# Turning the identity on TensorE ahead of the first keys, which come in two loads and are scored in two parts

## The chip, the core and the metric

The kernel runs on one core of a Trainium2 chip. The metric is the device time of one execution in microseconds (us); the lower the better.

## What is computed

Eight batches, eight heads of width 64, 576 tokens. A packed query p of 32 rows for each head first attends over the keys and values; then the 576 queries q attend over the 32 packed rows. The result, 4608 tokens by 512, goes through a feed-forward net with an ELU between its two matrices.

```python
def sm_attn(qq, kk, vv):
    s = scale * np.matmul(qq, kk.transpose(0, 1, 3, 2))
    s = s - np.max(s, axis=-1, keepdims=True)
    a = np.exp(s)
    a = a / (np.sum(a, axis=-1, keepdims=True) + 1e-09)
    return np.matmul(a, vv)
p_packed = sm_attn(p, k, v)            # (8, 8, 32, 64)
out = sm_attn(q, p_packed, p_packed)   # (8, 8, 576, 64)
x = out.transpose(0, 2, 1, 3).reshape(4608, 512)
h = x @ w_in                           # (4608, 2048)
g = np.where(h > 0.0, h, np.exp(np.minimum(h, 0.0)) - 1.0)
return (g @ w_out).astype(np.float32)
```

The weights arrive as float64, two 32-bit words each, and the kernel makes float32 of them.

## The kernel before

The work is written as some thousands of small steps. Each is an `op(prio, on, fn, deps, take, use, after)`: a priority, the engines that can do it with a cost for each, the function that issues its instructions, the steps it needs, the buffers that it takes and uses. `schedule()` is a planner: it plays the steps through in its own time with these costs, each time the first step in order of priority whose needs and buffers are there, and so fixes for every engine the order of its instructions. The instructions then stand on their engine's queue in that order, and each waits for what it needs. SP's queue issues nearly all loads.

The names that matter here, with the lines of the kernel before:

- `weights(f, first, prio)` turns one block of float64 weights into float32. Load `raw` (L305; three buffers, so the fourth load waits until the first block is used up), then on DVE `exponent` (L310), `mantissa` (L325), `whole` (L331), `signed` (L338) and `product` (L348), on ACT `sign` (L322) and `power` (L317). Blocks of the first matrix are called i0, i1, ..., of the second o0, o1, ... The blocks o0 to o3 are kept in `w_words` and later split into a high part (ACT, L282, CAST `wo_a`) and a low part (DVE, L361).
- `attention(b, ts)` is one batch. Loads of p and the keys (L459, L461 for batch 0, L463 for the others), the values (L470, L474) and the queries (L480, L482). Keys, values and queries of the batches after the first take turns in the same pairs of buffers (`kvq`), so that the queries of batch 1 are loaded when the values of batch 1 are used up.
- In it `s1` scores the packed queries (PE, L511). `smax1` (DVE, L521), `neg` (L529), `sexp1` (ACT, L535) and `srec1` (L543, L546) are its softmax, `tr1` turns it (PE, L622), ACT copies it (L282), `pv` multiplies by the values (PE, L648), `norm` scales (L660), and `tr2` (PE, L674) and a copy on ACT give `ppT`.
- `s2` scores one half of the queries against `ppT` (PE, L693). On DVE `fold` (L701), `smax` (L708), `ssub` (L711), on ACT `sexp` (L717), on DVE `ssum` (L721), `srec` (L724, L727), `smul` (L730) and `unfold` (L743) make the attention weights of that half.
- `mstep` multiplies `ppT` by the first matrix (PE, L794, copied by ACT as `m_hi`).
- The large matmuls of the net: L1263 and L1270 give a block of h (its first ones read what L743 wrote and `m_hi`), ACT and DVE make g of it (L1277, L1283, L1286), L1380 and L1394 to L1397 multiply it by the second matrix. In the later batches L1036 and L1175 do the same in another form.

The constants set priorities: `T_ATT1` the steps of batch 1 against the large matmuls, `LI`, `LO`, `LM` how long ahead weights and `mstep` come, `T_S2` the scores of batch 0's queries, `T_WS` the splitting of o0 to o3, `T_AS` the splitting of the first batches' attention weights. `FIRST` is the order of the first loads.

Of the kernel before, what the change touches and what calls it, by code (L numbers as in the profile page):

```python
# [20 lines left out]
def packed_attention_elu_ffn(  # L21
# [22 lines left out]
    nc = tc.nc  # L44
    B, P, NPAIR, S = qT.shape
# [32 lines left out]

    T_ATT, T_ATT1 = [12, 14.0, 14.5, 15.5, 16.5, 16.5], [-12, -11, -11, -10, -10, -9]
    LI, LO, LM, LOOK = 4.5, 3.0, 2.5, 3.5
    TM = [24.5, 22.0, 25.0, 25.5]

    FIRST = "i0 i1 i2 i3 k v o0 o1 q".split()
    T_S2, STAY, SWITCH = 0, 4, 0.12

    F_PLAIN, H_PLAIN = 4, [0, 1]  # L90
    T_WS, T_AS = 20, 6

# [64 lines left out]
    def op(prio, on, fn, deps=(), take=(), use=(), after=(), mode=None, lag=0):  # L159
        o = Op()  # L160
        o.lag = lag
        o.prio, o.on, o.fn, o.deps = prio, on, fn, [d for d in deps if d is not None]
        o.after = [d for d in after if d is not None]
        o.take, o.end, o.n, o.mode = list(take), None, len(ops), mode
        for b in list(take) + list(use):
            b.users.append(o)
        ops.append(o)
        return o
# [71 lines left out]
    ident = const.tile([P, P + 16], F32, name="ident")[:, 16:]  # L240
# [20 lines left out]
    def banks(n):  # L261
        b = Buf(R["psum"], lambda: psum[:, b.at, :] if n == 1 else psum[:, b.at:b.at + n, :], n)
        return b
# [137 lines left out]
    def attention(b, ts):  # L401
# [55 lines left out]
        def load_k(e, n):  # L457
            if n == 0:
                nc.sync.dma_start(out=p_b.t, in_=pT[b])  # L459
            if b == 0:  # L460
                nc.sync.dma_start(out=k_b[0].t, in_=kT[b])  # L461
            else:
                nc.sync.dma_start(  # L463
                    out=k_b[n].t[:, :2 * S].rearrange("p (c s) -> p c s", c=2),
                    in_=kT[b, :, 2 * n:2 * n + 2, :],
                )
# [21 lines left out]
        for name, fn, bufs, t in (  # L488
            ("k", load_k, k_b, ts[0] - 6), ("v", load_v, v_b, ts[0] - 5), ("q", load_q, q_b, ts[0] - 3),
        ):  # L490
            lds[name] = []
            if b == 0:
                t = FIRST.index(name) - 60
            for n, x in enumerate(bufs):
                prev_ld = op(
                    t, {"DMA": (3.3 if b < 3 else 3.8) / len(bufs)}, lambda e, fn=fn, n=n: fn(e, n),
                    take=[x] + ([p_b] if (name, n) == ("k", 0) else []), after=[prev_ld],
                    lag=1.5 * (b > 2),
                )
                lds[name].append(prev_ld)  # L500
        ld_k, ld_v, ld_q = lds["k"], lds["v"], prev_ld
# [2 lines left out]
        ps1, e1s = [banks(2) for _ in range(G)], [temp() for _ in range(G)]  # L504
        sv = {}

        def s1(e):
            for half in range(2):
                for pair in range(NPAIR):
                    for g in range(G):  # L510
                        nc.tensor.matmul(  # L511
                            ps1[g].t[cols_of(pair), half, :HS],
                            lhsT=p_b.t[rows_of(g), pair, :],
                            rhs=keys(pair)[rows_of(g), half * HS:(half + 1) * HS],
                            start=True, stop=True,
                        )
# [66 lines left out]

        o4s, o, t, free = [], None, ts[0], prev_b.tmp_last if b > 1 else None
        if b < S_FIRST[0] + 1:
            o1 = op(t, {"PE": 1.0}, s1, ld_k, take=ps1 + e1s, use=[p_b] + k_b, after=[free], mode=1)
            for g in range(G):
                o = op(t, {"DVE": 0.76}, lambda e, g=g: smax1(e, g), [o1], use=[ps1[g]], after=[o])
                o = op(t, {"DVE": 0.16}, lambda e, g=g: neg(e, g), [o])
                o4s.append(op(  # L590
                    t, {"ACT": 0.95}, lambda e, g=g: sexp1(e, g), [o], use=[ps1[g], e1s[g]],
                ))
        else:
            kept, o1 = [], None
            for half in range(2):
                ps = ps1[half]
                o1 = op(
                    t, {"PE": 0.52}, lambda e, half=half, ps=ps: s1_half(e, half, ps), ld_k,
                    take=[ps] + (e1s if half == 0 else []), use=[p_b] + k_b + e1s * half,
                    after=[free, o1], mode=1,  # L600
                )
                o = op(t, {"DVE": 0.76}, lambda e, half=half, ps=ps: smax1_half(e, half, ps), [o1],
                       use=[ps], after=[o])
                kept += [op(
                    t, {"ACT": 0.4}, lambda e, half=half, ps=ps, g=g: keep(e, half, ps, g), [o1],
                    use=[ps, e1s[g]],
                ) for g in range(G)]
            o = op(t, {"DVE": 0.26}, neg_both, [o])
            for g in range(G):
                o4s.append(op(  # L610
                    t, {"ACT": 0.9}, lambda e, g=g: sexp1_flat(e, g), [o] + kept[g::G], use=[e1s[g]],
                ))
# [398 lines left out]
    def strassen_pair(i, b, win, f):  # L1011
# [180 lines left out]
        if last:  # L1192
# [45 lines left out]

            op(q, {"DMA": 1.4}, store, [y], use=[part])

    acc = None
    for i, (b, win, f) in enumerate(order):
        st = sts[b]
# [252 lines left out]
```

## Time and profile before

| | |
|---|---|
| median of 3 runs | 713.93 us (713.62 to 714.21) |
| the profiled execution | 714.56 us, of which the span from the first to the last instruction is 712.4 us |
| busy share of the span | PE 97%, PEld 80%, DVE 81%, ACT 62%, POOL 3% |
| chain that ended last | PE 93%, DMA 3%, DVE 2%, ACT 1% |
| mean granted TensorE clock | 0.998 |

PE is TensorE's matmul and PEld its weight load, DVE VectorE, ACT ScalarE, POOL GpSimd and SP the queue that issues loads. The profile is one execution, so its rows add up to its own 714.56 us. A row of the timeline has start, length, engine, line, operation and tiles, and in brackets how long the engine was idle before it and what ended that. A row of the chain has start, length and what ran. Matmuls are pipelined, so the length of one (some 400 ns) is more than its share of a row of many.

### The profile page before, as it was taken

The page shows a single profiled execution, that of the slowest core. Times are in us where ns is not written, and L with a number is a line of the kernel's source. Part 1 is how long each engine was busy: PE and PEld are TensorE (multiplying, and loading weights), DVE is VectorE, ACT ScalarE, POOL GpSimd, SP SyncE. Part 2 cuts the span into 40 slices and gives each one's busy share as a digit, 9 for nine tenths or more (in the row PEclk, how much of TensorE's full clock was granted, in tenths as well). Part 3 has the DMA queues.
Part 4 walks back from the last instruction along what each step waited for, and adds up shares of the span by engine and source line. Part 5 has one row for each costly group of instructions (what it writes and reads, how often), then busy time and mean ns, then how long its engine had stood idle before and what let it go on. Part 6 is the DMA issues. An engine that isn't in the chain of part 4 may idle for free.

```text
span 712.4 us, 14951 instructions
## 1 busy us (share of the span) xinstructions
PE 689.7 (97%) x5616; PEld 572.2 (80%) x5616; DVE 576.4 (81%) x1405; ACT 442.2 (62%) x952; POOL 19.5 (3%) x27
## 2 busy tenths in 40 slices
PE   2799999999999999999999999999999999999997
PEld 1454588887778888988888988889888998899986
DVE  6999998888998899776996789776797789886553
ACT  5777788886666566665556455656556455655432
POOL 0000002111021000000000000000000000000000
PEclk9999999999999999999999999999999999999999
DMA  9846555545748836538577784627857874644400
GB/s 352 289 152 216 169 172 120 141 82 126 212 104 216 276 127 188 167 121 254 197 226 232 243 298 146 203 78 241 269 164 225 256 244 133 226 133 124 158 31 29
DMA packets 67368, 130.74 MB, mean 184 GB/s; under 512 B 6624, under 2 KB 16096, under 8 KB 67040
## 3 DMA queue, kind: packets, MB, share of 16 engines
q1 hardware_dynamic: 64272, 124.28, 53.6%
q0 software_dynamic: 3024, 5.51, 5.2%
q8 instruction: 44, 0.72, 0.4%
q14 instruction: 28, 0.23, 0.1%
HBM read 108.53 MB, written 21.23 MB: 182 GB/s over the span
## 4 chain that ended last, share of the span: by engine, by line
PE 93%; DMA 3%; DVE 2%; ACT 1%; issue 0%; SPq 0%; ACTq 0%
PE psum L1175 29%; PE psum L1036 18%; PE psum L1270 8%; PE psum L1394 5%; PE psum L1395 5%; PE psum L1397 5%; PE psum L995 5%; PE psum L794 4%; PE psum L1380 4%; PE psum L1263 2%; PE psum L648 1%; PE psum L622 1%; PE psum L693 1%; DMA out<-part 1%; DMA k<-in_kT 1%; PE psum L552 1%
## 5 line engine op out<-in xcount | busy, mean ns | idle before, releaser
L1175 PE MATMUL psum<-sw,g 128*128 128x256 f32 x720 | 112.3, 284 | 0.2
L1175 PEld LDWEIGHTS psum<-sw,g 128*128 128x128 f32 x720 | 96.7, 189 | 8.4 <-issue 6.4
L1036 PE MATMUL psum<-a_hi,m_hi 128*128 128x320 f32 (+1 forms) x320 | 96.9, 303 | 0.0
L1036 PE MATMUL psum<-a_lo,m_hi 128*128 128x320 f32 (+1 forms) x320 | 95.4, 298 | 0.0
L1036 PE MATMUL psum<-a_hi,m_lo 128*128 128x320 f32 (+1 forms) x320 | 95.3, 298 | 0.0
L282 ACT CAST g<-w 128x896 fp32r<-128x896 f32 (+1 forms) x80 | 68.6, 859 | 37.7 <-DVE w L1109 19.9
L1118 DVE TENSOR_TENSOR g<-w,g 128x896 fp32r<-128x896 f32 (+1 forms) x80 | 78.7, 985 | 16.1 <-ACT g L282 15.4
L1175 PE MATMUL psum<-wo_b,g 128*128 128x256 f32 (+1 forms) x390 | 72.7, 317 | 0.0
L1175 PE MATMUL psum<-wo_a,g 128*128 128x256 f32 (+1 forms) x390 | 72.2, 317 | 0.0
L1036 PEld LDWEIGHTS psum<-a_hi,m_hi 128*128 128x128 f32 x320 | 60.4, 189 | 11.3 <-issue 4.3
L1048 ACT ACTIVATE e<-psum 128x320 f32<-128x320 f32 x96 | 41.4, 436 | 43.4 <-PE psum L1036 33.9
L1277 ACT ACTIVATE e<-psum 128x256 f32<-128x256 f32 (+1 forms) x96 | 38.6, 403 | 46.9 <-PE psum L1270 32.9
L1175 PEld LDWEIGHTS psum<-wo_a,g 128*128 128x128 f32 x390 | 58.6, 188 | 7.7 <-issue 1.3
L1175 PEld LDWEIGHTS psum<-wo_b,g 128*128 128x128 f32 x390 | 58.5, 188 | 7.0 <-issue 2.6
L1109 DVE TENSOR_TENSOR w<-w 128x128 f32<-128x128 f32 x180 | 60.0, 334 | 4.4
L1036 PEld LDWEIGHTS psum<-a_lo,m_hi 128*128 128x128 f32 x320 | 60.4, 189 | 2.2
L1036 PEld LDWEIGHTS psum<-a_hi,m_lo 128*128 128x128 f32 x320 | 60.5, 189 | 0.0
L1043 DVE SCALAR_TENSOR_TENSOR w<-e,psum 128x256 f32<-128x256 f32 x96 | 39.7, 414 | 16.0 <-ACT e L1051 15.3
L1270 PE MATMUL psum<-a_hi,m_hi 128*128 128x256 f32 (+1 forms) x160 | 49.1, 307 | 0.0
L1286 DVE SCALAR_TENSOR_TENSOR e<-e,psum 128x256 f32<-128x256 f32 (+1 forms) x80 | 33.9, 425 | 16.1 <-ACT e L1283 15.9
L1270 PE MATMUL psum<-a_lo,m_hi 128*128 128x256 f32 (+1 forms) x160 | 46.4, 290 | 0.0
L1270 PE MATMUL psum<-a_hi,m_lo 128*128 128x256 f32 (+1 forms) x160 | 46.4, 290 | 0.0
(140 smaller groups left out, 1442.6 us busy)
## 6 DMA issues: line engine op xcount, KB each, us to landing
sw<-sw_dram SPq DMA_DIRECT2D x240, 256.0 KB, 3.6
raw<-in_w_in SPq DMA_DIRECT2D x16, 512.0 KB, 3.7
kvq<-in_v SPq DMA_DIRECT2D x16, 512.0 KB, 5.7
raw<-in_w_out SPq DMA_DIRECT2D x16, 512.0 KB, 3.5
kvq<-in_kT SPq DMA_DIRECT2D x14, 576.0 KB, 4.9
kvq<-in_qT SPq DMA_DIRECT2D x14, 576.0 KB, 5.0
sw_dram<-sw SPq DMA_DIRECT2D x24, 256.0 KB, 3.9
out<-part POOLq DMA_DIRECT2D x21, 256.0 KB, 5.3
```

What stands on the lines that cost most here:

```text
L282: (nc.scalar.copy if e == "ACT" else nc.vector.tensor_copy)(out=out, in_=in_)
L995: nc.tensor.matmul(acc.t, lhsT=gh.t[:, p * P:(p + 1) * P], rhs=wo(f, q), start=f == n == 0, stop=f == NF - 1 and n == 2,)
L1036: nc.tensor.matmul(ps, lhsT=m_b[p].t[:, g, o:o + P], rhs=st.a.t[q][:, g, cols], start=(n == 0), stop=(n == 3 * G - 1),)
L1043: nc.vector.scalar_tensor_tensor(out=out, in0=e_, scalar=-1.0, in1=ps, op0=ALU.add, op1=ALU.max)
L1048: nc.scalar.activation(out=out, in_=ps, func=AF.Relu, scale=-1.0)
L1109: nc.vector.tensor_tensor(out=out, in0=x, in1=y, op=o)
L1118: nc.vector.tensor_tensor(out=g_b.all[:, 7 * P:(7 + b1 - b0) * P], in0=blocks(b0, b1), in1=g_b.all[:, :(b1 - b0) * P].bitcast(F32), op=ALU ...
L1175: nc.tensor.matmul(a.t[:, at * H:at * H + rhs.shape[-1]], lhsT=operand(blk, p), rhs=rhs, start=a.first == u and n == k == 0, stop=a.final ...
L1270: nc.tensor.matmul(ps_b.t[:, :n_tok], lhsT=m_b[x].t[:, g, o:o + P], rhs=st.a.t[y][:, g, cols], start=(n == 0), stop=(n == 3 * G - 1),)
L1277: nc.scalar.activation(out=e_b.t[:, :n_tok], in_=ps_b.t[:, :n_tok], func=AF.Relu, scale=-1.0)
L1394: nc.tensor.matmul(a.t, lhsT=g_b.t[0][:, t], rhs=wo(f, 0), start=first, stop=False)
L1395: nc.tensor.matmul(a.t, lhsT=g_b.t[0][:, t], rhs=wo(f, 1), start=False, stop=False)
```

## The change

The identity matrix is turned 40 times on PE, into a bank of its own, as PE's first work. The keys of batch 0 come in two loads of two pairs of heads each, and `s1` of batch 0 becomes two steps, one for each load. Several constants of the planner are set anew, by which the order of instructions moves in about the first third of the program.

```diff
-    T_ATT, T_ATT1 = [12, 14.0, 14.5, 15.5, 16.5, 16.5], [-12, -11, -11, -10, -10, -9]
-    LI, LO, LM, LOOK = 4.5, 3.0, 2.5, 3.5
+    T_ATT, T_ATT1 = [12, 14.0, 14.5, 15.5, 16.5, 16.5], [-12, -11, -12, -11, -11, -10]
+    LI, LO, LM, LOOK = 5.5, 2.5, 2.0, 3.5
...
-    T_S2, STAY, SWITCH = 0, 4, 0.12
+    N_IDLE = 40
+    T_S2, STAY, SWITCH = 1, 4, 0.12
...
-    T_WS, T_AS = 20, 6
+    T_WS, T_AS = 17, 7.5
...
             if b == 0:
-                nc.sync.dma_start(out=k_b[0].t, in_=kT[b])
+                nc.sync.dma_start(
+                    out=k_b[0].t[:, 2 * n:2 * n + 2, :], in_=kT[b, :, 2 * n:2 * n + 2, :]
+                )
...
+            bufs = bufs * 2 if (b, name) == (0, "k") else bufs
             for n, x in enumerate(bufs):
+                old = x in bufs[:n]
                 prev_ld = op(
                     t, {"DMA": (3.3 if b < 3 else 3.8) / len(bufs)}, lambda e, fn=fn, n=n: fn(e, n),
-                    take=[x] + ([p_b] if (name, n) == ("k", 0) else []), after=[prev_ld],
-                    lag=1.5 * (b > 2),
+                    take=[x] * (not old) + ([p_b] if (name, n) == ("k", 0) else []),
+                    use=[x] * old, after=[prev_ld], lag=1.5 * (b > 2),
                 )
...
-        def s1(e):
+        def s1(e, pairs=range(NPAIR)):
             for half in range(2):
-                for pair in range(NPAIR):
+                for pair in pairs:
...
-            o1 = op(t, {"PE": 1.0}, s1, ld_k, take=ps1 + e1s, use=[p_b] + k_b, after=[free], mode=1)
+            if b == 0:
+                for n, ld in enumerate(ld_k):
+                    o1 = op(
+                        t, {"PE": 0.5}, lambda e, n=n: s1(e, range(2 * n, 2 * n + 2)), [ld],
+                        take=[] if n else ps1 + e1s, use=[p_b] + k_b + (ps1 + e1s) * n,
+                        after=[o1] if n else [free], mode=1,
+                    )
+            else:
+                o1 = op(
+                    t, {"PE": 1.0}, s1, ld_k, take=ps1 + e1s, use=[p_b] + k_b, after=[free], mode=1
+                )
...
+    idle_b = banks(1)
+    def turn_identity(e):
+        for _ in range(N_IDLE):
+            nc.tensor.transpose(out=idle_b.t[:, :P], in_=ident, identity=ident)
+    op(-100, {"PE": 7.0}, turn_identity, take=[idle_b], mode=0)
```

Where the order of instructions moves is shown at three places. Line numbers of the changed kernel are higher by 1 to 26: its L306, L462 and L473 are L305, L461 and L470 above, L311 to L362 are L310 to L361, L718 to L760 are L701 to L743, L1289 and L1406 are L1263 and L1380.

SP's queue, the first loads (`raw` is a block of weights, `k` the keys of batch 0, `kvq` here their values), before:

```order
L305 DMA raw<-in_w_in 128x1024 x3
L459 DMA p<-in_pT 128x128
L461 DMA k_123<-in_kT 128x2304
L305 DMA raw<-in_w_in 128x1024
L470 DMA kvq<-in_v 128x2x512
```

and in the changed kernel:

```order
L306 DMA raw<-in_w_in 128x1024 x3
L460 DMA p<-in_pT 128x128
L462 DMA k_163<-in_kT 128x1152
L306 DMA raw<-in_w_in 128x1024
L462 DMA k_163<-in_kT 128x1152
L473 DMA kvq<-in_v 128x2x512
```

The fourth load of weights (i3) stands behind all keys before, and between their two halves now.

DVE behind the `product` of o1, where the softmax of batch 0's first half of queries begins (`tmp<-psum` is its `fold`, `wo_a` the low part of o0 or o1), before:

```order
L348 SCALAR_TENSOR_TENSOR w_words<-mi,ex 128x512
L701 STREAM_TRANSPOSE tmp<-psum 128x288
L310 TENSOR_SCALAR ex<-raw 128x512
L701 STREAM_TRANSPOSE tmp<-psum 128x288
L325 TENSOR_SCALAR mi<-raw 128x512
L708 TENSOR_REDUCE mx_343<-tmp 128x18
```

and in the changed kernel:

```order
L349 SCALAR_TENSOR_TENSOR w_words<-mi,ex 128x512
L362 TENSOR_TENSOR wo_a<-w_words,wo_a 128x512
L311 TENSOR_SCALAR ex<-raw 128x512
L326 TENSOR_SCALAR mi<-raw 128x512
L362 TENSOR_TENSOR wo_a<-w_words,wo_a 128x512
L718 STREAM_TRANSPOSE tmp<-psum 128x288
L332 SCALAR_TENSOR_TENSOR mi<-raw,mi 128x512
L718 STREAM_TRANSPOSE tmp<-psum 128x288
```

Two low parts and two steps of o2 stand ahead of the first `fold` now; before, one low part stood behind it and the other after the whole half.

PE around `tr2` of batch 1 (`k_404` and `k_460` are the attention weights of batch 0, `kvq,tmp` is `pv` of batch 1 and `kvq,ppT` its `s2`), before:

```order
L648 MATMUL psum<-kvq,tmp 32x64 x40
L1263 MATMUL psum<-k_404,m_hi 128x256 x2
L674 MATMUL psum<-ident,pp 128x128
L1380 MATMUL psum<-w_words,g 128x512 x2
L1263 MATMUL psum<-k_404,m_hi 128x256 x2
L1380 MATMUL psum<-w_words,g 128x512 x2
L693 MATMUL psum<-kvq,ppT 32x288 x16
```

and in the changed kernel:

```order
L665 MATMUL psum<-kvq,tmp 32x64 x40
L1289 MATMUL psum<-k_460,m_hi 128x256 x2
L691 MATMUL psum<-ident,pp 128x128
L1406 MATMUL psum<-w_words,g 128x512 x2
L710 MATMUL psum<-kvq,ppT 32x288 x8
L1289 MATMUL psum<-k_460,m_hi 128x256 x2
L1406 MATMUL psum<-w_words,g 128x512 x2
L710 MATMUL psum<-kvq,ppT 32x288 x8
```

The two halves of `s2` stood together behind both pairs of L1263 and L1380; now the first half stands ahead of the second pair and the second half behind it.

## The prediction

> **What bounds the kernel now.** I read the table of busy time by stretch first, then the chain that ended last, then the rows of single engines and loads on it. In the table the columns are the stretch, its length, busy time of PE, PEld, DVE, ACT and POOL (instructions in brackets), the granted clock, the DMA share and GB/s.
>
> ```profile
> 0.00:20.00 20.00, 7.04 (x122) 4.76 (x122) 14.45 (x35) 11.54 (x21) 0.69 (x6) 1.00 0.91 357
> 20.00:30.00 10.00, 5.41 (x110) 2.47 (x102) 9.17 (x21) 6.93 (x15) 0.00 (x0) 1.00 0.96 338
> 30.00:40.00 10.00, 9.35 (x108) 6.78 (x108) 8.95 (x22) 8.00 (x21) 0.00 (x0) 0.83 0.63 202
> 40.00:60.00 20.00, 20.00 (x126) 9.04 (x125) 19.43 (x46) 13.36 (x27) 0.00 (x0) 1.00 0.50 171
> 60.00:80.00 20.00, 19.85 (x90) 10.69 (x89) 19.14 (x41) 16.63 (x36) 0.00 (x0) 1.00 0.52 172
> 700.00:712.40 12.40, 8.37 (x42) 6.65 (x40) 3.42 (x9) 2.57 (x6) 0.00 (x0) 1.00 0.12 42
> ```
>
> PE is full from 40 us (20.00 of 20) to the end. So there is nothing to win later: a change can only move the moment at which PE fills, and any new wait of PE after that costs its whole length. Ahead of 40 us DVE is the busy engine (9.17 of 10). The chain (start, length, what) and four timeline rows show how they hang together:
>
> ```profile
> 2.60 7.35 DMA k<-in_kT
> 10.09 2.27 PE psum L511 x32
> 20.48 0.66 ACT sg L322
> 30.68 1.32 PE psum L622 x5
> 12.34 0.76 DVE L521 TENSOR_REDUCE mx<-psum 128x1 f32<-128x576 f32 x1 [0.89 <-PE psum L511]
> 21.16 0.42 DVE L338 TENSOR_TENSOR ex<-ex,sg 128x512 bf16<-128x512 bf16 x1 [0.76 <-ACT sg L322]
> 30.22 0.77 DVE L743 STREAM_TRANSPOSE k<-tmp 128x576 f32<-128x576 f32 x1
> 31.80 2.84 PE L1263 MATMUL psum<-k,m_hi 128*128 128x256 f32 x8
> ```
>
> The keys land at 9.95, their scores are done at 12.34, and from there to the end of L743 (30.99) DVE works in one row, with one idle piece of 0.76 that an ACT instruction causes. L743 gives the attention weights that the first large matmuls (L1263, 31.80) read; from there PE stays full. So the length of DVE's list between L521 and L743 counts, not PE's speed.
>
> **The change, part by part.** The 40 turns of the identity. PE idles until 10.09 anyway, so they cost nothing as long as they end before the keys are needed. Their price and the clock:
>
> ```profile
> 1.02 0.29 POOL masks.py:199 TENSOR_SCALAR_AFFINE_SELECT ident<-ident 128x128 f32<-128x128 f32 x1
> L511 PE MATMUL psum<-kvq,p x64: 402/403/427, 25.2 to 169.9; 64*32 64x288 f32 x64
> L511 PE MATMUL psum<-k,p x32: 657/684/686, 10.1 to 11.6; 64*32 64x288 f32 x32
> 25.18 1.51 PE L511 MATMUL psum<-kvq,p 64*32 64x288 f32 x32 [1.05 <-ACT m_hi L282]
> 15.05 2.37 PE L622 MATMUL psum<-ident,tmp 128*128 128x128 f32 x10 [2.79 <-ACT tmp L535]
> 29.30 0.76 PE L622 MATMUL psum<-ident,tmp 128*128 128x128 f32 x5 [2.61 <-ACT tmp L535]
> 30.00:31.00 1.00, 0.38 (x3) 0.32 (x3) 1.00 (x3) 1.00 (x3) 0.00 (x0) 0.65 1.03 349
> 31.00:32.00 1.00, 1.00 (x6) 0.96 (x5) 0.97 (x5) 0.97 (x4) 0.00 (x0) 0.50 0.95 357
> 33.00:34.00 1.00, 1.00 (x4) 0.79 (x3) 1.00 (x3) 0.48 (x3) 0.00 (x0) 0.64 0.08 27
> ```
>
> The first scores take 684 ns a matmul where the next batch's take 403: PE starts at a low clock, though the column shows 1.00 there (it only knows changes). Ten turns take 2.37 at that speed, about 0.22 each; at full speed five take 0.76, about 0.12 each. The identity is made by 1.31, so forty need 4.9 to 8.7 us from about 1.4 us on, and end between 6.3 and 10.1; DVE, ACT and the loads don't wait for PE until then.
>
> The keys in two loads. On SP the load of i3 stands between the halves, and the row of i3 is
>
> ```profile
> 6.05 0.33 SPq L305 DMA_DIRECT2D raw<-in_w_in  x1
> raw<-in_w_in SPq DMA_DIRECT2D x1, 512.0 KB, 5.2
> 8.00:9.00 1.00, 0.00 (x0) 0.00 (x0) 1.00 (x3) 0.79 (x2) 0.00 (x0) 1.00 1.00 424
> ```
>
> i3 must wait for a free buffer (6.05) and lands at 11.25, behind the keys. At 424 GB/s half of the keys (0.59 MB) takes 1.4 us, i3 1.24. So the first half lands at about 8.5, i3 at 9.8, the second half at 11.2: the same bytes in another order. The keys are complete 1.3 us later than now. Left to do then is half the scores: (1.51-0.40)/31x15+0.40 = 0.94 us at full clock, 1.41 at the low one by the same sum from 2.18 and 0.68. L521 starts at 12.3 (12.8 if the clock is low) instead of 12.34. I take 0.0, bound +0.5: what the warm clock wins the later keys take. The extra issue on SP pushes the values back by some 0.35 us; they queue behind the same bytes.
>
> DVE from L521 to the end of L743. The order has 42 instructions there instead of 40: one more L361 and one more L331 (o1's low half, o3's words). L310 and L325 are as many as before (those of i3 go ahead of L521 into the 0.89 us in which DVE now idles, those of o3 come in). From start to start:
>
> ```profile
> 15.43 0.20 ACT L535 ACTIVATION_READ_ACCUMULATOR tmp<-psum,nb 128x1 f32 x1
> 16.20 0.16 DVE L543 TENSOR_SCALAR ri<-sm 128x2 f32<-128x2 f32 x1
> 17.25 0.69 DVE L331 SCALAR_TENSOR_TENSOR mi<-raw,mi 128x512 f32<-128x512 uint32 x1
> 17.86 0.42 DVE L310 TENSOR_SCALAR ex<-raw 128x512 uint16<-128x512 uint16 x1
> 25.90 0.68 DVE L361 TENSOR_TENSOR wo_a<-w_words,wo_a 128x512 fp32r<-128x512 f32 x1
> 26.50 0.74 DVE L721 TENSOR_REDUCE sm<-tmp 128x18 f32<-128x576 f32 x1
> ```
>
> L331 0.61 and L361 0.60: +1.21. ACT's signs of o1 now stand ahead of the batch's norms, so the 0.76 of idle goes: -0.76. New waits: L543 is reached some 0.75 sooner (two instructions of 0.42, like the L310 shown, go from ahead of it: 15.45), but the second exponential comes 0.27 later (L331 stands where L310 stood ahead of its bias), its sum at 15.9: +0.45. L521 of batch 1 waits for scores that stand behind a later L701 (two casts go ahead of ppT on ACT, two L361 ahead of L701 on DVE): about +0.25, an estimate. L743 ends at 30.99+1.21-0.76+0.45+0.25 = 32.14, L1263 follows at 32.19 against 31.80: **+0.4** (bounds -0.3 with none of the new waits, +0.9 with L521 0.5 later).
>
> Queries of batch 1 on PE. The order puts the first half of s2 (L693) ahead of two L1263 and two L1380 that stood before it:
>
> ```profile
> 35.99 0.31 ACT L660 ACTIVATE pp<-psum,ri 128x64 f32<-128x64 f32 x1 [0.62 <-PE psum L648]
> 36.06 1.34 SPq L482 DMA_DIRECT2D kvq<-in_qT  x2
> kvq<-in_qT SPq DMA_DIRECT2D x1, 576.0 KB, 4.2
> 37.29 1.88 PE L1380 MATMUL psum<-w_words,g 128*128 128x512 f32 x4
> 39.01 1.03 PE L1263 MATMUL psum<-k,m_hi 128*128 128x256 f32 x4
> 41.69 1.20 PE L693 MATMUL psum<-kvq,ppT 64*32 64x288 f32 x32
> 21.34 0.72 PE L693 MATMUL psum<-q,ppT 64*32 64x288 f32 x16 [0.37 <-ACT ppT L282]
> ```
>
> The load of these queries is issued when pv (L648) frees its buffers (35.99, issue 36.06) and lands 4.2 us later, at 40.26. PE's work from pv to the end of the first L1380s ends at 39.17. Now nothing is late, since s2 comes at 41.69. After the change PE stands at s2 from 39.17 to 40.3 with some 2.5 us of ready work (L1263 and L1380, now from 39.17 to 41.69) behind it: **+1.1**, wherever the whole block lies, since pv sets both ends. Bounds 0 (the work before it stretches) and 1.3. DVE's L701 and L743 of the other half wait behind it, which PE reaches only later.
>
> Split groups. Two halves of s2 apart cost 2x0.72 instead of 1.20: 0.24. The order of PE shows three more groups of small matmuls alone between large ones than before (this and two of L794): **+0.7** (bounds 0, if a lone group hides behind the large ones, and twice that). The other moved costs (weights' times, T_AS, T_WS) only reorder within the full stretch; PE covers them, and without that cover they add. From about a third of the program on the order is the same.
>
> Clock at the first large matmuls. It is 0.50 from 30.3 to 33.7 in the rows above, after PE's idle time; eight L1263 took 2.84 there against two times 1.03 later: 0.8 lost. The change leaves PE the same gap: 0, bounds -0.8 (no drop) and +1.7 (3.4 us more at half).
>
> [...] In this trace the ten turns from 15.05 on all run at the low price, and none of the rows shows turns alone that bring the clock up. [...]
>
> Sum: 0.4+1.1+0.7 = 2.2. The profiled execution took 714.56 (span 712.4 and 2.16 around it), 0.63 above the median 713.93; the difference is put on the median: **716.1**.
>
> **Rivals.** (a) The turns don't bring the clock up, so the change doesn't do what it says: scores at 1.41, L521 0.5 later, DVE's row with it: 716.6. For it: the row at 15.05. (b) The clock comes back 3.4 us later, because PE's restart falls otherwise: 1.7 more, 717.8. [...] (c) Not slower: the queries are in time, because PE's work before s2 stretches or the load is quicker; it decides if the landing comes within 3.2 us of pv's end: 2.2-1.1, 715.0. Against it: 4.2. (d) The first chain hangs on PE after all: turns 2.37 against 2x0.76 and a shorter pv let L743 end 2 us sooner: -2.2+1.8, 713.5; from an end of L743 before 29.5. Against it: DVE's 0.76 of idle in 18.65. (e) As (d), and the queries in time: 712.4, faster.
>
> **Chances.** Forecast 0.42, (a) 0.13, (b) 0.12, (c) 0.18, (d) 0.08, (e) 0.07. About 0.2% (1.43 us) is what a measurement can tell from no change. (c), (d) and the forecast's low edge (0.05) are the same: 0.31; (e) faster: 0.07; the rest slower: 0.62. The range leaves out (e) and the far end of (b): 713.4 (d) to 717.9 (b). The forecast's own range is 715.4 to 716.8.
>
> **What would show it.** Scores of the first keys at 403 ns a matmul (warm) or 684; the second half of k landing after i3, near 11.2; L743's first end at 32.1; PE idle about 1 us ahead of s2 of batch 1, put down to the load; PE full after that. Wrong if L743 ends before 31, if that PE wait is missing, or if the half-clock stretch moves.

## The result, and the profile after

The changed kernel takes 720.51 us (median of 4 runs, 718.83 to 720.91) against 714.07 (713.62 to 714.43) beside it: ratio 1.0077, 95% interval 1.0055 to 1.0098. It is 0.8% slower; 716.1 was predicted, 713.4 to 717.9 as the range. The profiled execution took 720.89, its span is 718.7 against 712.4 us, so its rows have 6.3 us to explain.

Rows of the timeline of the changed kernel, in the form of those shown of before: turns, scores, DVE's reductions, first large matmuls, the issue of batch 1's queries and their scores.

```profile
1.36 7.00 PE L1263 MATMUL psum<-ident 128*128 128x128 f32 x40 [1.36 <-POOL ident masks.py:199]
...
8.71 1.17 PE L517 MATMUL psum<-k,p 64*32 64x288 f32 x16 [0.36 <-DMA k<-in_kT]
...
11.97 1.18 PE L517 MATMUL psum<-k,p 64*32 64x288 f32 x16 [2.09 <-DMA k<-in_kT]
...
13.20 0.76 DVE L527 TENSOR_REDUCE mx<-psum 128x1 f32<-128x576 f32 x1 [1.23 <-PE psum L517]
...
16.64 0.17 DVE L549 TENSOR_SCALAR ri<-sm 128x2 f32<-128x2 f32 x1 [0.30 <-ACT tmp L541]
...
29.04 0.76 DVE L527 TENSOR_REDUCE mx<-psum 128x1 f32<-128x576 f32 x1 [1.20 <-PE psum L517]
...
33.09 0.77 DVE L760 STREAM_TRANSPOSE k<-tmp 128x576 f32<-128x576 f32 x1
...
33.92 3.53 PE L1289 MATMUL psum<-k,m_hi 128*128 128x256 f32 x8 [0.59 <-DVE ri L549]
...
38.87 1.84 SPq L485 DMA_DIRECT2D kvq<-in_qT  x2
...
43.16 0.72 PE L710 MATMUL psum<-kvq,ppT 64*32 64x288 f32 x16 [1.42 <-DMA kvq<-in_qT]
...
47.23 2.42 PE L1289 MATMUL psum<-k,m_hi 128*128 128x320 f32 x8
```

Loads in the chain that ended last (start, length):

```profile
6.39 5.54 DMA k<-in_kT
...
21.04 6.73 DMA kvq<-in_kT
...
38.87 4.15 DMA kvq<-in_qT
```

The turns end at 8.36 and the scores run fast, but the second half of the keys lands at 11.93, so the scores are done at 13.15, later than before. Batch 1's second keys land at 27.77, and DVE waits 1.20 for their scores. Two rows of before that were not shown give the marks to compare:

```profile
27.17 0.75 DVE L521 TENSOR_REDUCE mx<-psum 128x1 f32<-128x576 f32 x1
...
42.82 2.42 PE L1263 MATMUL psum<-k,m_hi 128*128 128x320 f32 x8
```

| mark | before | after | difference |
|---|---|---|---|
| first reduction of batch 0's scores | 12.34 | 13.20 | +0.86 |
| first reduction of batch 1's scores | 27.17 | 29.04 | +1.87 |
| first large matmul | 31.80 | 33.92 | +2.12 |
| eight of them take | 2.84 | 3.53 | +0.69 |
| first 320-wide large matmul | 42.82 | 47.23 | +4.41 |
| from that one to the end | 669.6 | 671.5 | +1.9 |

PE has the same work ahead of the first 320-wide matmul in both orders, so 4.41 is 2.12 for the later start, 0.69 for the clock, 1.42 of wait for the queries, and 0.18 for s2 in two groups and the rest. The last 1.9 us are lost later; together these are the 6.3. The waits of PE behind 40 us (sum, times, longest):

```profile
PE psum L710 <- DMA kvq<-in_qT: 1.4, 1, 1.4
PE psum L1053 <- DVE part L1216: 0.9, 1, 0.9
PE psum L665 <- DMA kvq<-in_v: 0.7, 1, 0.7
PE psum L665 <- DVE w L921: 0.2, 1, 0.2
```

Before, the same list has 0.2 us in all. Busy time by stretch says it in another way (columns as in the prediction's first table; of before first): PE has 652.65 us of work left at 60 us where it had 647.90, and idles 6.05 us in it where it idled 4.50.

```profile
60.00:712.40 652.40, 647.90 (x5163) 549.13 (x5161) 524.43 (x1286) 402.38 (x869) 18.76 (x21) 1.00 0.58 176
```

and of the changed kernel:

```profile
60.00:718.70 658.70, 652.65 (x5187) 550.41 (x5185) 528.96 (x1293) 405.45 (x874) 18.66 (x21) 1.00 0.59 176
```

### The profile page after: what moved, and what is told of

Its sections match the earlier page's. It is cut to its first block, busy times and chain, and to the rows that moved or that the text cites. A ratio compares the mean times of both kernels' runs of the same rounds, so it can differ in the third digit from the quotient of the medians.

```text
span 718.7 us, 15052 instructions
## 1 busy us (share of the span) xinstructions
PE 699.3 (97%) x5656; PEld 578.6 (80%) x5656; DVE 578.2 (80%) x1406; ACT 442.6 (62%) x951; POOL 19.4 (3%) x27
## 4 chain that ended last, share of the span: by engine, by line
PE 92%; DMA 4%; DVE 2%; ACT 1%; issue 0%; SPq 0%; ACTq 0%
PE psum L1192 29%; PE psum L1053 18%; PE psum L1296 8%; PE psum L1420 5%; PE psum L1421 5%; PE psum L1423 5%; PE psum L1012 5%; PE psum L811 4%; PE psum L1406 4%; PE psum L1289 2%; PE psum L665 2%; PE psum L710 1%; DMA kvq<-in_v 1%; DMA kvq<-in_kT 1%; PE psum L639 1%; PE psum L558 1%
## 5 line engine op out<-in xcount | busy, mean ns | idle before, releaser
L283 ACT CAST g<-w 128x896 fp32r<-128x896 f32 (+1 forms) x80 | 68.6, 859 | 37.4 <-DVE w L1126 19.8
L1296 PE MATMUL psum<-a_lo,m_hi 128*128 128x256 f32 (+1 forms) x160 | 46.4, 290 | 0.0
L1296 PE MATMUL psum<-a_hi,m_lo 128*128 128x256 f32 (+1 forms) x160 | 46.4, 290 | 0.0
L1068 ACT ACTIVATE e<-e 128x320 f32<-128x320 f32 x96 | 44.5, 472 | 2.2
```

The lines of the kernel that those rows point to most:

```text
L283: (nc.scalar.copy if e == "ACT" else nc.vector.tensor_copy)(out=out, in_=in_)
L1068: nc.scalar.activation(out=x, in_=x, func=AF.Exp, scale=-1.0)
L1296: nc.tensor.matmul(ps_b.t[:, :n_tok], lhsT=m_b[x].t[:, g, o:o + P], rhs=st.a.t[y][:, g, cols], start=(n == 0), stop=(n == 3 * G - 1),)
```

## The experiments

Each was timed in five rounds beside the kernel before on its chip; the ratio is against that. The medians of before there were 714.18 (old_constants to halves_together below), 715.55 (change_without_turns and the three with late turns), 714.39 (halves_no_turns, second_half_behind, change_halves_together, change_queries_later), 714.69 (change_max_first, change_load_behind, change_bare, turns_in_gap) and 714.63 (max_first_no_turns, halves_and_gap), so ratios are to be compared, not medians. The two marks are of one profiled execution each: when the first 320-wide matmul starts, and how long it is from there to the end of the span. "Before" in the column of the order means that every row but those named stands as in before.

| run | order | ratio (95%) | 320-wide | rest |
|---|---|---|---|---|
| before | before | 1 | 42.8 | 669.6 |
| halves_no_turns | before | 1.0005 (0.9990 to 1.0020) | 43.7 | 668.8 |
| turns_only | before | 1.0052 (1.0036 to 1.0067) | 44.8 | 669.1 |
| halves_together | before | 1.0029 (1.0012 to 1.0047) | 44.2 | 669.3 |
| second_half_behind | before | 1.0036 (1.0022 to 1.0050) | 47.2 | 668.9 |
| late_turns | before | 1.0020 (1.0002 to 1.0037) | 45.0 | 668.8 |
| turns_throughout | before | 1.0056 (1.0035 to 1.0077) | 47.3 | 670.0 |
| turns_in_gap | before | 0.9990 (0.9974 to 1.0007) | 44.0 | 669.6 |
| halves_and_gap | before | 0.9997 (0.9985 to 1.0009) | 42.2 | 670.2 |
| new_constants | its own | 1.0028 (1.0013 to 1.0043) | | |
| old_constants | its own | 1.0084 (1.0066 to 1.0103) | | |
| the change | change | 1.0077 (1.0055 to 1.0098) | 47.2 | 671.5 |
| change_without_turns | change | 1.0078 (1.0051 to 1.0106) | 47.9 | 670.6 |
| change_late_turns | change | 1.0097 (1.0067 to 1.0126) | 50.5 | 671.1 |
| change_halves_together | change | 1.0063 (1.0041 to 1.0086) | 46.4 | 672.2 |
| change_queries_later | change | 1.0052 (1.0032 to 1.0072) | 47.1 | 670.8 |
| change_max_first | change | 1.0038 (1.0020 to 1.0056) | 45.1 | 670.6 |
| max_first_no_turns | change | 1.0060 (1.0041 to 1.0080) | 46.2 | 670.3 |
| change_load_behind | change | 1.0060 (1.0038 to 1.0083) | 46.5 | 669.6 |
| change_bare | change | 1.0063 (1.0038 to 1.0088) | 47.5 | 670.8 |

### The constants and the parts by themselves

old_constants: the change with the constants of before; the planner then finds an order of its own.

```diff
...
-    LI, LO, LM, LOOK = 5.5, 2.5, 2.0, 3.5
+    LI, LO, LM, LOOK = 4.5, 3.0, 2.5, 3.5
...
-    T_WS, T_AS = 17, 7.5
+    T_WS, T_AS = 20, 6
```

> The changed kernel (turns of the identity, keys in two loads with i3 between them, scores in two parts) with the planner's seven constants of the kernel before. Theory 1, the order of instructions costs the time, most of it by the constants: the wait of PE for the queries of batch 1 (1.4 us before s2) and the late keys of batch 1 (DVE idle 1.2 us) go, what stays is the later first scores (second half of the keys at 11.9 instead of 9.95, L521 0.9 later) and what the planner makes of the two steps: 714.5 to 716.5. Theory 2, the turns themselves cost the time by the swings of the clock: still 719 to 721. Theory 3, the two loads cost it all: also 719 to 721, but with the first large matmul over 1.5 us late.

720.03 us, as slow as the change. new_constants, the reverse: before with the new constants, one load and no turns.

> The kernel before with the seven constants of the changed one, without the turns, the keys in one load and their scores in one step. Theory 1 (the order that the constants make): 717 to 719.5, with waits of PE after 40 us like those of the changed kernel (s2 of batch 1 for its queries, batch 1's keys late). Theories 2 and 3 (turns or loads): 713.5 to 715, as the kernel before.

715.41 against 714.18, between the theories. So the constants are not all that makes the change slow: they cost 0.28% alone, and with those of before the split kernel, in the order that the planner then finds, is no faster.

turns_only: the order of before with the 40 turns ahead.

```diff
+    idle_b = banks(1)
+    def turn_identity(e):
+        for _ in range(40):
+            nc.tensor.transpose(out=idle_b.t[:, :P], in_=ident, identity=ident)
+    op(-100, {"PE": 7.0}, turn_identity, take=[idle_b], mode=0)
```

> The kernel before with the 40 turns alone; the order of all other instructions is the same on every engine. Theory 1: first scores at 403 ns instead of 684 a matmul, so L521 starts some 0.9 us sooner (11.4); but DVE works in one row from there, and reaches the weights' steps that it would have done anyway; L743 ends up to 0.9 us sooner, and PE, which the turning of batch 1 holds until 31.6, gains 0 to 0.9: 713.0 to 714.2. Theory 2 (the turns cost by the clock): 716 and more. Rival of both, the chain hangs on PE's speed and the turns win 2 us: 712.

717.02 us; the gain did not come, and the time lies in the range of theory 2. halves_together adds two key loads side by side and two-part scores (the loads are shown):

```diff
-                nc.sync.dma_start(out=k_b[0].t, in_=kT[b])
+                for n in range(2):
+                    nc.sync.dma_start(
+                        out=k_b[0].t[:, 2 * n:2 * n + 2, :], in_=kT[b, :, 2 * n:2 * n + 2, :]
+                    )
...
```

> As turns only, and the keys in two loads issued one behind the other with i3 behind both, the scores in two parts within one step; the order of all instructions but this load is that of the kernel before. Theory 1: the second half lands where all keys land now (9.95), half of the scores is left, L521 starts at 11.0 to 11.4 as DVE is busy to 11.45 anyway: at most some 0.2 us better than turns only, 712.8 to 714.2. Theory 3 (two loads cost): over 716, with the keys landing later than 10.5.

716.19, slower than theory 1 allows; but the second half of the keys landed at 10.04, so theory 3 does not explain it either. Here are the rows of turns_only behind the turns:

```profile
11.26 0.75 DVE L521 TENSOR_REDUCE mx<-psum 128x1 f32<-128x576 f32 x1
...
26.31 2.14 PE L511 MATMUL psum<-kvq,p 64*32 64x288 f32 x24 [1.08 <-DMA kvq<-in_kT]
...
28.51 0.76 DVE L521 TENSOR_REDUCE mx<-psum 128x1 f32<-128x576 f32 x1 [1.57 <-PE psum L511]
...
33.16 3.26 PE L1271 MATMUL psum<-k,m_hi 128*128 128x256 f32 x8
```

The reduction of batch 0 starts 1.08 us earlier (11.26 for 12.34), that of batch 1 1.34 later (28.51 for 27.17): what the clock won is gone before the first large matmul. PE waits 1.08 for keys, and then is not warm: the 24 matmuls behind that wait take 2.14, where new_constants has the same 24 in 1.17. The clock (third from the end) shows why, first in turns_only, then in before:

```profile
27.00:30.00 3.00, 1.46 (x23) 0.19 (x4) 1.46 (x5) 0.90 (x2) 0.00 (x0) 0.50 0.84 272
30.00:32.00 2.00, 1.33 (x5) 0.87 (x5) 2.00 (x5) 1.45 (x5) 0.00 (x0) 0.50 0.99 363
32.00:34.00 2.00, 1.97 (x7) 1.75 (x8) 1.97 (x8) 1.97 (x5) 0.00 (x0) 0.50 0.41 148
```

```profile
27.00:30.00 3.00, 0.70 (x5) 0.50 (x5) 2.97 (x9) 1.69 (x4) 0.00 (x0) 1.00 1.02 374
30.00:32.00 2.00, 1.38 (x7) 1.28 (x7) 1.97 (x7) 1.97 (x6) 0.00 (x0) 0.58 0.99 353
```

In turns_only the clock is at half from 25.7 to 35.9 us (by its mean of 0.78 from 24 to 27 and 0.68 from 34 to 37), in before from 30.3 to 33.7.

halves_no_turns: halves_together without the turns.

> The kernel before with batch 0's keys in two loads that stand back to back where the one load stood, and its scores in two parts that follow each other; no turns, every other row as before. Theory C (the two loads and the two parts cost nothing by themselves; what costs is where the second load stands and which rows move with it): the ratio to before is 0.998 to 1.002. Theory D (two loads, or the parts' extra changes of shape, cost by themselves): 1.003 or more.

714.43 against 714.39: the split costs nothing by itself that the interval of 0.15% either way would show (theory C). second_half_behind: the second load behind i3, as in the change.

```diff
...
-                for n in range(2):
-                    k_half(n)
+                k_half(0)
+                later.append(lambda: k_half(1))
...
```

> The same with the second load issued behind the fourth w_in block, as in the change; nothing else moves and there are no turns. The second part of the scores then starts near 12.0 us and ends at half clock near 14.2, against 12.3 for the whole scores in before. Theory C1 (this place of the load sets the cost): DVE's row and the first large matmul move by the full 1.9 us, of which 1 to 1.9 reach the end: ratio 1.0015 to 1.003. Theory C2 (the delay is taken up by the waits that follow it, as for the keys that landed late in other runs; the cost of the change is in its other moved rows): within 0.1% of before.

716.26: 0.36%, a little above the range of theory C1. Its scores of batch 0 (second part) and its first large matmul:

```profile
13.03 2.15 PE L522 MATMUL psum<-k,p 64*32 64x288 f32 x16 [2.00 <-DMA k<-in_kT]
...
15.22 0.76 DVE L532 TENSOR_REDUCE mx<-psum 128x1 f32<-128x576 f32 x1 [3.87 <-PE psum L522]
...
35.60 3.46 PE L1275 MATMUL psum<-k,m_hi 128*128 128x256 f32 x8
```

The load landed about 1 us later than I had put it, and the reduction starts 2.88 later than in before; the first large matmul starts 3.80 later.

### Taking back the change's parts one by one

change_without_turns: the change with `range(0)` for `range(N_IDLE)`.

> The changed kernel with its 40 turns left out, every other row on every engine as in it. Theory A (the turns cost by themselves, as the 2.8 us of the 40 turns alone): 717.5 to 718.5 us. Theory B (the cost of the change is in the split keys and the moved rows; the turns only cost where there is no other wait): 720 to 721 us. In between, both share.

720.61, theory B: in the change's own order the turns are worth nothing that these intervals would show. They do win 1.1 us at batch 0's reduction (13.20 against the 14.30 below) and 0.44 at the first large matmul (33.92 against 34.36), yet the time is the same within the intervals.

```profile
14.30 0.76 DVE L527 TENSOR_REDUCE mx<-psum 128x1 f32<-128x576 f32 x1 [2.48 <-PE psum L517]
...
34.36 3.78 PE L1289 MATMUL psum<-k,m_hi 128*128 128x256 f32 x8
```

change_halves_together: both key loads ahead of i3.

```diff
-                nc.sync.dma_start(
-                    out=k_b[0].t[:, 2 * n:2 * n + 2, :], in_=kT[b, :, 2 * n:2 * n + 2, :]
-                )
+                for m in range(2 * (1 - n)):
+                    nc.sync.dma_start(
+                        out=k_b[0].t[:, 2 * m:2 * m + 2, :], in_=kT[b, :, 2 * m:2 * m + 2, :]
+                    )
```

> The changed kernel with the second load of the keys ahead of the fourth w_in block instead of behind it; no other row moves. The scores should end near 11.3 us instead of 13.1. Theory C1 (the place of the load is the larger part of the change's 6.4 us): 716.5 to 718. Theory C2 (the other moved rows are): 719 to 720.5, because PE still waits 1.4 us for batch 1's queries and DVE still has more rows between its reductions.

718.93 us, between the theories. The scores end at 11.27, but DVE's moved rows stand ahead of the reductions, and PE waits for the queries as in the change (rows of the timeline, then one of PE's waits behind 30 us):

```profile
10.09 1.18 PE L518 MATMUL psum<-k,p 64*32 64x288 f32 x16 [0.18 <-DMA k<-in_kT]
...
12.72 0.75 DVE L528 TENSOR_REDUCE mx<-psum 128x1 f32<-128x576 f32 x1
...
14.05 0.75 DVE L528 TENSOR_REDUCE mx<-psum 128x1 f32<-128x576 f32 x1
```

```profile
PE psum L711 <- DMA kvq<-in_qT: 1.7, 1, 1.7
```

change_queries_later adds the place of s2's first half, moved in the finished list of steps:

```diff
...
-        for o, e in schedule():
+        plan = schedule()
...
+        ends = [pe[1]] + [max(n for n in dve if plan[n][0].n < moved[0].n and n < pe[2])] * 2
...
+        for o, e in new:
```

> The kernel of the line above with one more edit: the first half of batch 1's score products with the queries stands behind four more w_words matmuls and two 256-wide ones, directly ahead of its second half, as in the order of before, and DVE's two folds of it stand behind batch 0's last multiply and fold. In the trace of the change PE waits 1.4 us for those queries; theory C3 (that wait is paid in full, since PE is full behind it): 1.3 to 1.5 us less than the kernel of the line above. Theory C4 (PE's wait only moves to the next rows): no change.

717.96, 0.97 us less by the medians, though the intervals overlap; less than theory C3 said. The wait of 1.7 us is gone from the list, and a part of it comes back at s2's second half, where PE waits for DVE's fold (the same view):

```profile
PE psum L711 <- DVE tmp L719: 0.6, 1, 0.6
```

change_max_first adds: the two reductions and `neg` directly behind the third `signed`.

```diff
...
+        signed = [n for n in range(s1_2) if new[n][0].fn.__name__ == "signed"][-1]
+        new = (new[:signed + 1] + pairs + [p for p in new[signed + 1:] if p not in pairs])
```

> The kernel change_queries_later with one more edit: DVE's two reductions of batch 0's scores and the two small rows behind them stand directly behind the third signed block, ahead of the rows of the fourth weight block that the change has ahead of and between them. In the trace the scores end at 11.2 us, and the reductions start at 12.6 and 13.9 us. Theory M (these moved rows are part of the change's cost): the reductions start at 11.2 and 12.3, and the first large matmul 1 to 1.5 us earlier, so 0.7 to 1.5 us less than that kernel's 717.96. Theory N (ACT's rows or the arrival of batch 1's keys set the start of the large matmuls): within 0.5 us of it.

Its reductions start at 11.33 and 12.19 and its first large matmul 0.72 earlier (32.84 for 33.56):

```profile
11.33 0.76 DVE L528 TENSOR_REDUCE mx<-psum 128x1 f32<-128x576 f32 x1 [0.58 <-PE psum L518]
...
32.84 3.12 PE L1294 MATMUL psum<-k,m_hi 128*128 128x256 f32 x8 [0.21 <-DVE ri L550]
```

The ratio falls from 1.0052 to 1.0038, but the intervals overlap widely and the median is 718.11 on another chip: the rows say M, the time does not settle it. change_load_behind adds: o3's load behind batch 1's keys.

```diff
...
+        last, at = new[dma[12]], dma[14]
+        new = new[:dma[12]] + new[dma[12] + 1:at + 1] + [last] + new[at + 1:]
```

> The kernel change_max_first with one more edit: the load of the fourth w_out block is issued behind batch 1's two key loads instead of ahead of them, as in before. In the trace batch 1's second keys land late, 0.3 us after PE could use them. Theory M: 0.3 to 1 us less than change_max_first. Theory N: no difference, since the keys' transfer takes as long whichever load stands ahead of it.

719.50, no gain (if anything a loss, 1.0060 for 1.0038). change_bare takes the turns out of that:

> The kernel change_load_behind without its 40 turns. Theory M (with the waits gone, the turns cost as they do in the order of before, 0.3 to 0.5%): 1.5 to 3 us less. Theory N (the turns are worth nothing either way, as in the change itself, where leaving them out changed nothing): within 0.7 us.

719.84 against 719.50, theory N. max_first_no_turns takes them out of change_max_first, without the moved load:

> The kernel change_max_first (718.11 us, ratio 1.0038) without its 40 turns; no other row moves. Theory P (what is left is the turns, as in the order of before, where they cost 0.2 to 0.5%): ratio 0.9995 to 1.002. Theory Q (what is left is the rows that the constants move, 0.28% by themselves; the turns are worth nothing, as in the change): 1.003 to 1.005.

718.94, ratio 1.0060 (1.0041 to 1.0080). That rules out theory P and lies above the range of Q; the turns are worth nothing here either, so what is left must lie mostly in the rows that the planner moved.

### What the clock is worth

late_turns: turns ahead of batch 1's two turnings of scores, in the order of before.

```diff
             def tr1(e, g=g, e1=e1, pt=pt):
+                for _ in range({(1, 0): 20, (1, 1): 5}.get((b, g), 0)):
+                    nc.tensor.transpose(out=pt.t[:, 0, :P], in_=ident, identity=ident)
```

> The kernel before, with 25 added turns of the identity (20 ahead of batch 1's first turning of scores, 5 ahead of the second), in the gap in which the trace of before has PE idle from 26.7 to 29.3 and from 30.1 to 30.7 us; no other row moves on any engine. [...] Theory B (arrivals of keys and queries and the DVE and ACT rows behind them set the time; the clock does not matter): no change, 713.9 to 714.4, or up to 715 if the turns delay the turnings.

716.89 us. The run did not do what I meant: the turns write the turning's own bank of PSUM, wait for ACT to leave it and run where the turning should.

```profile
29.16 3.96 PE L621 MATMUL psum<-ident 128*128 128x128 f32 x20 [2.32 <-ACT tmp L535]
...
34.59 1.89 PE L1265 MATMUL psum<-k,m_hi 128*128 128x256 f32 x8
```

The eight large matmuls take 1.89 instead of 2.84, so the clock does come up (1.00 from 34 to 60 us), but they start 2.79 later. The same fault was in change_late_turns (in the change) and in turns_throughout (before with the 40 turns, 20 and 4 turns more at batch 0's turnings, 20 and 5 at batch 1's):

> The changed kernel with 25 turns more, 20 and 5 ahead of batch 1's two turnings of scores (no other row moves). In the changed kernel's trace the half-clock stretch from 33.8 to 37.2 us holds eight large matmuls in 3.53 us and most of batch 1's value products. Theory A (the clock): full there, so 1.6 to 1.8 us less, 718.5 to 719.2 against 720.5. Theory B (keys and queries that land late decide): 720 to 721.

> The kernel before with the 40 turns at the start, and turns in the gaps of PE behind them as well: 20 and 4 ahead of batch 0's two turnings of scores, 20 and 5 ahead of batch 1's; no other row moves. With the 40 turns alone it took 717.0 us. Theory A (the 40 turns cost because PE then idles, and the half-clock stretches come to lie on the large matmuls): no half-clock stretch is left between 6 and 38 us, and the time falls below before: 712.5 to 713.5. Theory B (the 40 turns cost through something else, such as batch 1's keys that land 1 us later): the time stays at 716.5 to 717.3.

722.92 and 719.52 us. turns_in_gap repairs it: 8, 20 and 4 turns into a bank that is free until then.

```diff
...
+            if (name, seen[name]) == ("s1", 2):
+                turns(8)
...
             o.fn(e)
+            if (name, seen[name]) == ("s1", 2):
+                turns(20)
+            if (name, seen[name]) == ("tr1", 3):
+                turns(4)
```

> The kernel before with 32 turns into a bank of PSUM that nothing uses until then: 8 ahead of batch 1's scores, 20 behind them, 4 between its two turnings; each waits for nothing, and in before's trace PE idles 1.05, 2.61 and 0.62 us at these places; no turns at the start, no other row moves. Theory A (the clock): at full clock the turns take 0.9, 2.2 and 0.4 us and delay nothing, PE is busy up to the first large matmul, and no half-clock stretch lies on these: 0.9 to 1.1 us less than before (ratio 0.9985 to 0.9988) and less scatter between runs. Theory B (what the clock gives at the first large matmuls is taken back by a later wait): ratio 0.9995 to 1.0005.

714.34 against 714.69. Rows of its timeline, and then the longest of PE's waits behind 30 us:

```profile
28.49 2.40 PE L1455 MATMUL psum<-ident 128*128 128x128 f32 x20
...
32.74 1.89 PE L1263 MATMUL psum<-k,m_hi 128*128 128x256 f32 x8
...
36.73 1.13 PE L1263 MATMUL psum<-k,m_hi 128*128 128x256 f32 x4 [0.71 <-DVE g L1286]
```

```profile
PE psum L1263 <- DVE g L1286: 0.9, 2, 0.7
PE psum L674 <- ACT sw L282: 0.8, 1, 0.8
PE psum L693 <- DMA kvq<-in_qT: 0.5, 1, 0.5
```

The half clock is gone from the large matmuls (1.89 for 2.84, the clock 1.00 from 20 to 60 us), and PE then waits for DVE, for the queries and, later, for ACT: what the clock gives, the next wait takes back in this execution. By the interval of the times it is worth between 0.26% and nothing. What goes is the spread: its 12 executions all have a mean granted clock of 0.999 or 1.000 and spans of 711.1 to 713.6 us, while of the 27 of before beside them 8 have 0.993 or less, with a mean span of 715.2 (the other 19 have 712.3). halves_and_gap joins it with halves_no_turns:

> The order of before with batch 0's keys in two loads side by side, its scores in two parts, and the 32 turns in PE's gaps ahead of the first large matmuls; none at the start. By the two runs alone (1.0005 and 0.999): ratio 0.998 to 1.0005. If the DVE rows and the queries' load behind the first large matmuls take back what the clock gives, as in the run with the turns alone, it stays within 0.1% of before.

714.59 against 714.63. Its first 320-wide matmul starts 0.67 us ahead of that of before, and the span is the same 712.4 us: ACT (0.9) and a load (0.5) make PE wait later. No version beats the kernel before by more than its interval.

## Why the prediction was wrong

The direction was right (a chance of 0.62 for slower), the size was not: 2.2 us forecast, 6.3 in the profiled span. Of the 4.1 between them 1.7 lie ahead of the first large matmul, 0.7 in the clock there, 0.3 in the wait for the queries, and 1.4 in the split groups and moved rows. The steps in their order:

- **The turns** end at 8.36 (6.3 to 10.1 forecast), and the scores behind them run warm:

```profile
L517 PE MATMUL psum<-k,p x32: 399/402/427, 8.7 to 12.7; 64*32 64x288 f32 x32
```

  402 ns instead of 684 behind 40 float32 turns, so rival (a) falls. That the turns cost nothing holds in the change (1.0078 without them, 1.0077 with) and not in the order of before (1.0052).
- **The second half of the keys** landed at 11.93 instead of 11.2. The loads moved 360 and 381 GB/s from 8 to 12 us where 424 was put in:

```profile
8.00:10.00 2.00, 1.53 (x20) 0.61 (x18) 2.00 (x5) 1.33 (x2) 0.00 (x0) 1.00 1.01 360
10.00:12.00 2.00, 0.03 (x4) 0.03 (x4) 1.97 (x5) 1.27 (x2) 0.00 (x0) 1.00 0.98 381
```

  With 1.18 for the rest of the scores where 0.94 was forecast, the reduction came at 13.20, past the bound of 12.8. This place of the load costs 0.36% in the order of before.
- **DVE from L521 to L743: the step that failed most.** +0.4 (-0.3 to +0.9) was forecast for the first large matmul, +2.12 came. The row starts 0.86 later and takes 20.66 us instead of 18.65, so it ends 2.87 later (33.86 for 30.99); 0.75 of that does not reach PE, which before was still turning until 31.8. I counted the row to 19.8; nearly all of the 0.86 beyond that is the wait for batch 1's scores, 1.20 where 0.25 was put, less a shorter wait of L549 (0.30 where 0.45 was put). I had not followed batch 1's keys: their second load lands at 27.77, 6.73 us after its issue, and the last 24 matmuls of the scores start there. In before it landed at 25.47, 4.83 us after its issue.
- **The queries**: PE waits where it was said, 1.42 us for 1.1 (bound 1.3). Put back, about 1 us by the medians.
- **The clock** at the first large matmuls was put at 0 and cost 0.69 (bounds -0.8 to +1.7): the stretch at half moved from 30.3 to 33.7 us to 33.7 to 37.1, and so onto all eight of them, which the prediction had named as a sign of being wrong. turns_in_gap bounds what it is worth in the order of before: 0.26% at most.
- **Split groups and moved rows**: 0.7 for small groups, and "PE covers" the other moved rows. That cover was not there. s2 in two groups took 1.44 in its rows for 1.20, the 0.24 that was forecast, but from the first 320-wide matmul to the end the change takes 1.9 us more, 1.6 of it in waits of PE. In nine profiled executions with the order of before this stretch is 668.8 to 670.2 us, in nine with that of the change 669.6 to 672.2. One place is common: between 194 and 199 us `pv` of a later batch (L665) waits 0.3 to 0.8 us for its values in eight of these nine (in change_max_first `s2` waits 0.4 for queries just behind that place), and in none of the nine with the order of before. Which moved row does it is not settled: putting back the two that I could name (DVE's rows, o3's load) did not end it.

Rival (b), the clock by itself, came nearest with 717.8, but only by accident: its 1.7 us were 0.69. The queries landed 4.15 us after their issue, so (c) and (e) fall, and L743 (L760 now) ended at 33.86, so (d) falls too.

What stays open: why 40 turns cost 0.3 to 0.5% in the order of before. One profiled execution shows batch 1's keys late, but these land late in executions without turns at the start too (PE waits 1.39 us for them in second_half_behind, 0.44 in turns_in_gap). The clock is the nearer candidate: turns_only has 10.2 us at half over batch 1's scores and the first large matmuls, before has 3.4. Of the 104 executions of before beside the experiments, the 19 with a mean granted clock of 0.993 or less (10 us or more at half) have a median span of 715.0 us, the others 712.1; turns_only's median is 714.8. This fits, but it is not shown, since late keys also leave PE idle (1.08 us up to 26.31 in turns_only, where the half clock starts at 25.7); the run that would tell them apart, the 40 turns with turns in the later gaps that delay nothing, was not made.

## What to carry to other kernels

A clock that was warmed ahead of a wait was worth nothing behind it in the change (1.0077 with the turns, 1.0078 without): follow the whole chain to the point at which the busiest engine fills, here loads and DVE's list, before pricing a faster engine at its head. Splitting a load was free where both parts stood together (1.0005) and dear where another load came between (1.0036), since the step that needs both waits for the later one. And "the full engine covers the moved rows" must be checked for each wait behind the point of filling: behind it a wait can add in full, as most of the last 1.9 us did.

## What the runs showed of the hardware

The 40 turns of the identity ran at two speeds. In the change the 22 that start by 5.9 us have a median length of 421 ns (one starts every 0.22 us), the 18 from 6.1 us on 273 (every 0.12 us), so they become faster some 5 us after the first one. All of them took 7.00 us there, and 5.95 to 6.69 in six of the other runs that have them. The scores behind them take 402 ns a matmul (median) at 8.7 us, and still so at 12.0 us, behind a wait of 2.09 for keys. After these scores the clock is down (columns as above, the clock third from the end):

```profile
12.00:13.00 1.00, 1.00 (x16) 0.38 (x16) 0.00 (x0) 0.01 (x1) 0.00 (x0) 1.00 1.04 383
13.00:14.00 1.00, 0.15 (x4) 0.00 (x0) 0.80 (x2) 0.00 (x0) 0.00 (x0) 0.59 1.10 415
```

In that execution the clock is 0.50 from 13.2 to 20.0 us, from 23.4 to 26.8 and from 33.7 to 37.1, and 1.00 between these. Ahead of each PE was idle for a part of the time: it was busy for 0.03 of 2.00 us from 10 to 12 us, for 1.42 of 3.40 from 20.0 to 23.4, and for 0.50 of 2.00 from 30 to 32. In before it was busy for 0.70 of 3.00 us from 27 to 30, ahead of the half clock from 30.3 to 33.7; with turns in PE's gaps there (turns_in_gap) the clock is 1.00 from 20 to 60 us, and the eight large matmuls take 1.89 us instead of 2.84. So in these executions the first large matmuls paid for idle time of PE ahead of them.

How much idle time it takes was not shown. From 24 to 27 us PE was busy for 1.64 of 3.00 us in before, with the clock at 1.00, and for 1.38 in turns_only, where the mean clock of these 3 us is 0.78. From 27 to 30 us turns_only has 1.46 of 3.00 us and from 30 to 32 1.33 of 2.00, both at 0.50; why it stays at half to 35.9 us these figures do not settle.
